# Sums per head, a fixed order of operations, and GpSimd for the lower words of the weights

## The chip, the cores and the metric

The kernel runs on one core of one Trainium2 chip. The metric is the device time of one launch in microseconds (us). All inputs lie in HBM and the output is written there.

## The reference

Two blocks run one after the other. The first is attention with a polynomial sketch: batch 4, 4 heads, 1088 tokens, 32 numbers a head, sketch size 8.

```python
def phi(x):
    a = np.einsum('rd,bhsd->bhsr', S1, x)
    b = np.einsum('rd,bhsd->bhsr', S2, x)
    return np.einsum('bhsi,bhsj->bhsij', a, b).reshape(*x.shape[:-1], r * r)
q_p, k_p = phi(q), phi(k)
num = np.einsum('bhsf,bhfd->bhsd', q_p, np.einsum('bhsf,bhsd->bhfd', k_p, v))
den = np.einsum('bhsf,bhf->bhs', q_p, np.sum(k_p, axis=2))[..., None] + 1e-06
x = (num / den)                       # then (B, S, H*D)
```

The second is a token mix with phases, on 128 channels:

```python
theta = x @ w_theta
y = w_tok_r @ (x * cos(theta)) + w_tok_i @ (x * sin(theta))     # over the tokens
u = x + y
out = u + np.maximum(u @ w_ch, 0.0)
```

The denominator can come close to zero, so the kernel carries it in two or more words of precision. The weights arrive as 64-bit floats.

## The kernel before, in words

Tokens lie on the 128 partitions, in 9 chunks. Nothing loops on the chip: the program lists some 990 operations with `op(engine, duration, function, writes, reads)` and the class `Layout` puts them in one order before anything is issued. An operation is one or a few instructions of one engine: P is TensorE (PE), V VectorE (DVE), A ScalarE (ACT), G GpSimd (POOL), S the queue of loads and stores on SyncE (SP). Each engine works off its own instructions in that order. In the kernel before, the order comes from a planner with durations, due times, a table `SHIFT` of corrections by stage, and buffer classes with reserves (L102 to L294). Where the planner foresees that PE stands, `issue` puts filler matmuls on an idle tile (`spin`, L458).

What is computed, with the names used below:

- **Weight rows.** The token weights are 17 rows of 128 x 1088 64-bit floats (`weight`, L671). A row is loaded into a `zs` buffer, ScalarE makes the upper word (L678) and the scaled and rounded lower word (L680), both into `big` buffers; VectorE shifts the upper word (L682) and adds the lower one (L684, shown as CUSTOM_DVE_ANT_0 at L407).
- **Keys** (`key_sums`, L700). For every batch k is split into a rounded bf16 part and a remainder. `sums` multiplies the rounded part with itself, `rest` the remainder with k (batch 0 in two products, batches 1 to 3 with k plus the rounded part, which an accumulating DMA has added up). All are 128 x 128 products over all four heads, though only the four 32 x 32 blocks on the diagonal are needed. Two or three products with the identity (`both`, `three`) add the transposed result.
- **The chain** (`chain`, L873; batches 0, 1, and 2 with 3 together). From the key products it makes the sum of the key features, in several words: `split`, `first`, `split_t`, `second`, a maximum, `cut`. Its result goes into the tables `mv` and `mf`, which `levels` (L1065) multiplies with q. `den` then makes the denominators, some ten VectorE steps a batch.
- **Values** (`kfeatures`, L793). The products of key features and v; batches 0 and 1 do two heads in one matmul (`sums`), batches 2 and 3 one head (`sums4`), which makes 128 x 32 pieces of the array.
- **Numerators** (`outputs_x`, L1144): an outer product on VectorE, transposes and matmuls on PE. They give x, then `theta`: rounding, Abs and two Sin on ScalarE, two steps on VectorE, which give z, the operand of the mix.
- **The mix.** Batches 0 and 1 multiply z with the 17 rows, 1088 columns a row (`mix_row`, L1260). Batches 2 and 3 share seven half-size products (`winograd`, L1300); their sums of weights come from VectorE (`asub`, `zsub`) and from accumulating DMAs that GpSimd issues (`aadd`, L1326). `balance` (L1233) gives the ratio of scale between these two batches. `finish` (L1286) multiplies with `w_ch`, adds, transposes and stores.

Of the kernel before, what the change touches and what calls it, by code (L numbers as in the profile page):

```python
# [29 lines left out]
MIX = (49.7, 1.87, 0.654, 0.0)  # L30
ROWS = (55.0, 3.96)
RPS = 4
EARLY = (2, 60.0, 4.0)
SHIFT = {
    "ac1": 1959.7, "ac2": -34.2, "ac3": 16.2, "ac4": 82.9, "acc1_0": 42.2, "acc1_1": -2320.9, "acc2_0": 31.2,
    "acc2_1": -673.1, "acc3_0": 5.8, "acc3_1": 932.8, "acc4_0": 3.9, "acc4_1": 16520.4, "acc5_0": 161.3,
    "acc5_1": 16109.1, "acc6_0": -223.6, "acc6_1": -1014.6, "acc7_0": 535.5, "acc7_1": -1181.2, "accl3_0":
    -35.5, "accl3_1": 15950.9, "blocks_k": 270.7, "blocks_m": 14976.6, "blocks_t": 353.2, "chain0": -7990.2,
    "chain1": -3583.6, "chain2": 70.5, "den0": -2490.2, "den1": 7.9, "den2": -6608.0, "den3": -20.6, "even":
    -4802.9, "first": -3782.9, "grid0": 274.3, "grid1": -1356.4, "grid2": -2521.6, "grid3": -5645.2, "kT0":  # L40
    -487.7, "kT1": -2.4, "kT2": -8729.0, "kT3": -4586.2, "keys0": -517.6, "keys1": -3965.9, "keys2": 1185.2,
    "keys3": 57.5, "kf0": -4478.9, "kf1": 31.3, "kf2": 427.4, "kf3": 16536.5, "kv0": -6047.2, "kv1": -6685.9,
    "kv2": -2098.9, "kv3": -8834.4, "kvb0": -4690.2, "kvb1": -2155.7, "kvb2": 600.6, "levels0": 1123.4,
    "levels1": -4027.2, "levels2": -2720.9, "levels3": -51.7, "loadh1": -3105.3, "loadh2": 24.7, "loadh3":
    -32.1, "loadk0": -4069.2, "loadk1": -8392.7, "loadk2": -1144.9, "loadk3": -5199.7, "loadq0": -7696.5,
    "loadq1": -6262.4, "loadq2": -958.3, "loadq3": 55.1, "loadv0": -5952.5, "loadv1": -912.1, "loadv2": -207.4,
    "loadv3": -1494.9, "m1_0": -1842.0, "m2_0": -13.3, "m2_1": 16313.2, "m3_0": 18317.8, "m3_1": 15711.6,
    "m4_0": 16151.7, "m4_1": 16888.8, "m5_0": 15826.2, "m5_1": 32.4, "m6_0": 182.9, "m6_1": 15250.5, "m7_0":
    16773.6, "m7_1": 15963.6, "mix0_0": 2883.6, "mix1_0": 16498.2, "mix1_1": -20.5, "mix1_2": 16164.9, "num0_0":
    -10062.4, "num0_1": -6861.6, "num0_2": -17390.2, "num1_0": -4679.4, "num1_1": -4010.3, "num1_2": 1566.7,  # L50
    "num2_0": -3.1, "num2_1": 15934.4, "num2_2": -4056.8, "num3_0": 15737.7, "num3_1": 35.0, "num3_2": -1483.3,
    "out0_0": -3691.3, "out0_1": 1196.2, "out0_2": -1707.0, "out1_0": 15899.8, "out1_1": 17081.6, "out1_2":
    -518.5, "out2_0_0": 6.6, "out2_0_1": 137.0, "out2_1_0": 16969.9, "out2_1_1": 16164.5, "out3_0_0": 16314.5,
    "out3_0_1": -978.2, "out3_1_0": 15740.8, "out3_1_1": 15780.8, "q00": -4645.6, "q01": 396.0, "q02": 43.0,
    "q03": -3238.5, "qT0": -372.8, "qT1": 531.2, "qT2": 18716.0, "qT3": 15783.1, "qscale0": -879.3, "qscale1":
    -7112.5, "qscale2": -116.9, "qscale3": -21.6, "rest0": -3460.7, "rest1": 15824.3, "rest2": -7.2, "rest3":
    -936.2, "row0": -32.5, "row1": -8124.5, "row10": -0.1, "row11": -1.8, "row12": -1.0, "row13": -6489.0,
    "row14": -2.1, "row15": 4.5, "row16": 6.0, "row2": -652.5, "row3": -35.3, "row4": -1008.6, "row5": -5.4,
    "row6": -5.0, "row7": -5.9, "row8": -2280.6, "row9": -7.6, "scaled": -2734.1, "sliced": 16062.8, "small":
    -5354.8, "square2": -5038.6, "sums0": 16352.5, "sums1": 2269.4, "sums2": 18.2, "sums3": 15743.7, "theta0_0":  # L60
    -4953.6, "theta0_1": -2793.7, "theta0_2": -11.6, "theta1_0": -4079.1, "theta1_1": -5573.0, "theta1_2":
    -2865.1, "theta2_0": -27.0, "theta2_1": -1634.0, "theta2_2": -41.0, "theta3_0": -677.3, "theta3_1": 133.0,
    "theta3_2": 382.0, "w2": -2254.2, "zc1": 1851.7, "zc2": 117.5, "zc3": 11.2, "zc4": 16233.0,
}
WARM = 0
FILL = 5.0
LOAD_LEAD = 60.0
RAW_LEAD = 30.0
# [4 lines left out]
PAIR = (2, 3)  # L73
SMALL = (2, 3)
# [7 lines left out]
ADD_FLY3 = 1.45  # L82
# [15 lines left out]
class Op:  # L98
    __slots__ = ("eng", "dur", "fn", "bufs", "pred", "succ", "due", "wait", "ready", "start", "end", "i", "lead", "rank", "lk", "fly", "stage", "chan")


class Layout:  # L102
# [9 lines left out]
    HURRY = 100.0  # L112
    LAND = 1.1
    STORE = 0.9
    RESERVE = {"big": 8, "zs": 2, "lv": 0, "hf": 1, "g3": 3, "g1": 2, "sm": 4, "ps": RPS}
    SLACK = {"P": 0.05, "V": 0.25, "A": 0.25, "G": 0.25, "S": 0.4}
# [10 lines left out]
    def op(self, eng, dur, fn, w=(), r=(), due=None, hold=(), lead=1e9, lk=0, fly=0.0, chan=0.0):  # L127
        o = Op()
        o.lk, o.fly, o.stage, o.chan = lk, fly + (chan + self.LAND if chan else 0.0), self.stage, chan
        o.i, o.eng, o.dur, o.fn, o.due = len(self.ops), eng, dur, fn, 1e9 if due is None else due  # L130
        o.succ, pred, o.lead = [], set(), lead
# [35 lines left out]
        for p in o.pred:  # L167
            self.ops[p].succ.append(o.i)
# [3 lines left out]
    def lag(self, o, t):  # L172
        if o.eng == t.eng:
            return o.fly + self.SAME[o.eng]
        return o.fly + self.LAT[o.eng] + (self.WAKE if t.eng == "G" else 0.0)

    def run(self):
        for o in reversed(self.ops):
            for s in o.succ:
                t = self.ops[s]  # L180
                o.due = min(o.due, t.due - t.dur - self.lag(o, t))
        for o in self.ops:
            o.due += SHIFT.get(o.stage, 0.0)
        return self.forward()

    def forward(self):
        ops = self.ops
        for o in ops:
            o.wait, o.ready, o.rank = len(o.pred), 0.0, o.due
            if o.eng in "VA" and any(b.cls == "ps" for b in o.bufs):  # L190
                o.rank -= self.HURRY
        slots = {c: [[0.0, None, i] for i in range(n)] for c, (n, _) in self.classes.items()}
# [3 lines left out]
        ready = {e: [o for o in ops if o.eng == e and not o.wait] for e in "PVAGS"}  # L196
        order, done = [], 0

        pending = {c: [] for c in self.classes}
        for b in self.bufs:  # L200
            b.left, b.slot, b.end = len(b.ops), None, 0.0
            if b.cls is not None:
                b.due = min(ops[i].due for i in b.ops)
                pending[b.cls].append((b.due, b.ops[0], b))
        for v in pending.values():
            v.sort(key=lambda x: x[:2])

        def place(o, loose):
            t = 0.0
            need = {}  # L210
            for b in o.bufs:
                if b.slot is None and b.cls is not None:
                    need.setdefault(b.cls, []).append(b)
# [1284 lines left out]
```

## Time and profile before

| | |
|---|---|
| median of 3 runs | 236.32 us (236.29 to 236.84) |
| the profiled execution | 235.85 us |
| its span, first to last instruction | 234.0 us |
| mean granted TensorE clock | 0.984 |
| instructions | 4153 |
| moved by DMA | 40.13 MB, 171 GB/s over the span |

The span is what the trace covers; the profiled execution's time lies 1.8 us above it. A row in a view names the line, the engine, the operation, what it writes and reads, the shape, and how many instructions there are. A helper's line stands for all who call it: every matmul of `mm` is L427, every `tensor_tensor` L407, every `tensor_scalar` L411. An f32 matmul leaves two records.

### The profile page before, as it was taken

How to read it: one execution, taken by the hardware profiler on the slowest of the kernel's cores; microseconds unless marked ns; L12 is line 12 of the kernel's file. 1: busy time of each engine (PE TensorE's matmuls, PEld its weight loads, DVE VectorE, ACT ScalarE, POOL GpSimd, SP SyncE). 2: the span in 40 equal slices, each digit the busy share in tenths (PEclk: the TensorE clock that was granted, in tenths of full speed). 3: DMA queues.
4: the chain of work that ended last, by engine and by line, in shares of the span. 5: the costliest groups of instructions: out<-in, count | busy, mean ns of one | idle time of the engine just before them, and what ended most of it. 6: DMA issues, size and time to landing. Idle time of an engine off the chain costs nothing.

```text
span 234.0 us, 4153 instructions
## 1 busy us (share of the span) xinstructions
PE 222.0 (95%) x1557; PEld 171.0 (73%) x1557; DVE 173.2 (74%) x356; ACT 114.4 (49%) x223; POOL 57.3 (25%) x110
## 2 busy tenths in 40 slices
PE   7899979999999998999999999999999999989980
PEld 3798969998787655765668676776868888767860
DVE  3599958998989999999458989778957862522241
ACT  3898648779699974997343103580026420000000
POOL 2299705110140000000277042000008664000000
PEclk9999979999999999999999999999999999999996
DMA  4999999997641797050097986010006999951124
GB/s 135 415 413 413 356 406 413 340 310 232 251 132 61 286 385 283 0 193 1 11 146 105 237 133 104 3 29 3 0 0 100 177 187 169 188 85 31 16 41 65
DMA packets 28035, 40.13 MB, mean 171 GB/s; under 512 B 19568, under 2 KB 20336, under 8 KB 25840
## 3 DMA queue, kind: packets, MB, share of 16 engines
q1 hardware_dynamic: 23168, 30.29, 38.3%
q0 software_dynamic: 4752, 9.57, 23.0%
q8 instruction: 12, 0.20, 0.3%
q14 instruction: 7, 0.06, 0.1%
q10 hardware_dynamic: 96, 0.01, 0.0%
HBM read 28.07 MB, written 2.23 MB: 129 GB/s over the span
## 4 chain that ended last, share of the span: by engine, by line
PE 58%; DMA 21%; DVE 8%; issue 5%; POOL 4%; ACT 1%; SPq 1%; POOLq 0%; ACTq 0%
PE ps L427 53%; DMA big<-q_l 6%; DMA zs<-big 5%; DMA zs<-w_tok 5%; DMA big<-hf 4%; POOL zs L1329 2%; DVE big L407 2%; PE ps L1170 2%; DVE big L411 1%; POOL big L1329 1%; PE ps L1203 1%; DVE lv L407 1%; PE ps L1050 1%; DVE zs L407 1%; DVE big L414 1%
## 5 line engine op out<-in xcount | busy, mean ns | idle before, releaser
L427 PE MATMUL ps<-big,zs 128*128 128x384 f32 (+3 forms) x348 | 100.0, 439 | 0.6 <-DVE big L407 0.6
L427 PEld LDWEIGHTS ps<-big,zs 128*128 128x128 f32 x348 | 64.6, 190 | 29.2 <-DVE big L407 2.0
L407 DVE CUSTOM_DVE_ANT_0 big<-big,big 128x2176 uint16<-128x2176 uint16 x17 | 21.9, 1286 | 0.7
L680 ACT ACTIVATE big<-zs 128x1088 int32<-128x1088 uint32 (+1 forms) x18 | 21.0, 1175 | 0.0
L421 POOL DMA_DIRECT2D g<-big x6 | 8.0, 1335 | 52.0 <-ACT g L1280 51.8
L678 ACT ACTIVATE big<-zs 128x1088 f32<-128x1088 f32 x17 | 20.5, 1220 | 0.1
L427 PE MATMUL ps<-big,big 128*128 128x128 f32 (+2 forms) x104 | 19.3, 316 | 0.5 <-DMA big<-hf 0.5
L427 PEld LDWEIGHTS ps<-big,big 128*128 128x128 f32 x104 | 15.4, 192 | 2.3 <-DMA big<-hf 0.8
L414 DVE SCALAR_TENSOR_TENSOR big<-ps,even,big 128x256 f32<-128x256 f32 (+1 forms) x10 | 5.0, 497 | 14.8 <-PE ps L427 14.8
L1329 POOL DMA_DIRECT2D big<-zs x8 | 7.0, 2064 | 32.1 <-PE ps L427 32.1
L407 DVE TENSOR_TENSOR zs<-ps,g 128x768 f32<-128x768 f32 (+2 forms) x20 | 12.2, 626 | 3.3 <-ACT g L1218 3.2
L427 PE MATMUL ps<-mf,big 128*128 128x96 f32 x72 | 14.3, 295 | 0.0
L411 DVE TENSOR_SCALAR big<-big 128x1088 int32<-128x1088 int32 x17 | 12.1, 719 | 0.4 <-ACT big L678 0.3
L427 PEld LDWEIGHTS <-hf 128*128 128x128 f16 (+1 forms) x144 | 11.1, 104 | 1.5 <-issue 0.9
L1141 ACT COPY big<-ps 128x288 f32<-128x288 f32 x8 | 2.6, 413 | 18.3 <-PE ps L427 18.3
L407 DVE TENSOR_TENSOR g<-lv 128x768 f32<-128x768 f32 x12 | 11.1, 946 | 0.1
L407 DVE TENSOR_TENSOR big<-big,hf 128x1152 f32<-128x1152 f32 x8 | 10.8, 1353 | 0.1
L427 PEld LDWEIGHTS ps<-mf,big 128*128 128x128 f32 x72 | 10.9, 191 | 0.0
L427 PE MATMUL ps<-mv,hf 128*128 128x96 f16 x108 | 10.5, 206 | 0.0
L427 PEld LDWEIGHTS ps<-w,big 128*128 128x128 f32 x72 | 9.3, 192 | 1.4 <-ACT big L1183 0.6
L427 PE MATMUL ps<-g,big 128*32 128x64 f32 (+1 forms) x216 | 8.9, 255 | 1.5 <-ACT sm L831 1.5
L427 PE MATMUL ps<-w,big 128*128 128x128 f32 x72 | 10.0, 277 | 0.0
(199 smaller groups left out, 410.3 us busy)
## 6 DMA issues: line engine op xcount, KB each, us to landing
zs<-w_tok SPq DMA_DIRECT2D x17, 1088.0 KB, 7.7
big<-k_l SPq DMA_DIRECT2D x7, 576.0 KB, 14.6
big<-q_l SPq DMA_DIRECT2D x4, 576.0 KB, 10.1
big<-v_l SPq DMA_DIRECT2D x4, 576.0 KB, 14.9
big<-big POOLq DMA_DIRECT2D x8, 272.0 KB, 7.0
big<-zs POOLq DMA_DIRECT2D x8, 272.0 KB, 8.9
zs<-big POOLq DMA_DIRECT2D x8, 272.0 KB, 10.3
big<-hf POOLq DMA_DIRECT2D x3, 576.0 KB, 9.2
```

The lines of the kernel that those rows point to most:

```text
L407: eng.tensor_tensor(out=o, in0=a, in1=b, op=f)
L411: (eng or V).tensor_scalar(out=o, in0=a, scalar1=s1, scalar2=s2, op0=op0, **kw)
L414: (eng or V).scalar_tensor_tensor(out=o, in0=a, scalar=s, in1=b, op0=op0, op1=op1)
L421: op("G", 0.9, lambda: G.dma_start(dst(), src(), accum_op=ALU.add), w, r, chan=chan)
L427: T.matmul(o, lhs, rhs, start=start, stop=stop, skip_group_check=True)
L678: op("A", 0.22 + n * 0.0009, lambda: A.activation(dfn(), words_of(raw(), n)[1].bitcast(F32), AF.Prelu, scale=2.0**-112, alpha=-(2.0**32)), ...
L680: op("A", 0.22 + n * 0.0009, lambda: A.activation(stp(), words_of(raw(), n)[0].bitcast(U32), AF.Copy, scale=2.0**-29), [stp], [raw])
L1050: T.transpose(tr()[:, i * P:(i + 1) * P], x()[:, g * GC + i].rearrange("p h d -> p (h d)"), ident())
L1141: op("A", act(NC * SQ), lambda i=i: A.copy(xt().rearrange("p (c q t) -> p c q t", q=NQ, t=SQ)[:, :, i], xps[i]()), cells(xt, 0, NC * P), [ ...
L1170: T.transpose(tr()[:, i * P:(i + 1) * P], qp()[:, i * H + 2 * n:i * H + 2 * n + 2].rearrange("p h i j -> p (h i j)"), ident())
L1203: T.transpose(x()[:, i], xs()[:, off + i * P:off + (i + 1) * P], ident())
L1329: op("G", 0.9, lambda i=i: G.dma_start(dst[0](i), x[0](i), accum_op=ALU.add), [dst[1](i)], [x[1](i)], chan=ADD_FLY3)
```

## The change

The diff has five parts.

1. **Order.** The planner with its due times is gone. A list `ORDER` of all 993 operation numbers, in the order of their calls, is followed as it stands; the remaining model in `run` serves the choice of buffers and the filler.
2. **Key sums per head.** `sums` and `rest` make four 32 x 32 products a chunk. The products with the identity go; `split` transposes the blocks on VectorE instead.
3. **Compact chain.** The intermediate results hold 8 columns a batch where there were 32, since each head lies on its own partitions; `first` becomes narrow matmuls, the mask is applied later, in `norms` and `cut`.
4. **Values.** Batches 0 and 1 also take one head a matmul.
5. **Lower words.** For weight rows 4 to 16 GpSimd scales and rounds the lower word, for the others ScalarE still does.

In `balance`, VectorE's two maxima become two squares with a sum on ScalarE. Loads are queued in another order, and so are the accumulating DMAs. `QBLOCK` is empty, so its branch is not taken.

```diff
+LOW = tuple(range(4, 17))
...
     def run(self):
-        for o in reversed(self.ops):
-            for s in o.succ:
-                t = self.ops[s]
-                o.due = min(o.due, t.due - t.dur - self.lag(o, t))
-        for o in self.ops:
-            o.due += SHIFT.get(o.stage, 0.0)
-        return self.forward()
...
+        seq = [int(x) for x in ORDER.split()]
...
+        self.order = [ops[i] for i in seq]
...
+        if low:
+            op("G", 0.06 + n * 0.00115, lambda: ts(stp(), words_of(raw(), n)[0].bitcast(U32), 2.0**-29, ALU.mult, eng=G),
+               [stp], [raw], lk=1)
+        else:
+            op("A", 0.22 + n * 0.0009, lambda: A.activation(stp(), words_of(raw(), n)[0].bitcast(U32), AF.Copy,
+                                                         scale=2.0**-29), [stp], [raw])
...
-        t = kk[b] = buf("ps", (4, HD), F32, "kk")
+        t = kk[b] = buf("ps", (3, D), F32, "kk")
+
+        def heads(i, x, y, start, stop):
+            for h in range(H):
+                e = slice(h * D, (h + 1) * D)
+                mm(t()[e, i], x[:, e], y[:, e], start, stop)
+
         for c in range(NC):
-            op("P", 0.056, lambda c=c: mm(t()[:, 0], kb()[:, c], kb()[:, c], c == 0, False), [(t, "l")], [kb])
+            op("P", 0.1, lambda c=c: heads(0, kb()[:, c], kb()[:, c], c == 0, False), [(t, "l")], [kb])
...
-            def both():
-                mm(t()[:, 2], g()[:, 1], ident(), False, False)
-                mm(t()[:, 2], ident(), g()[:, 1], False, True)
...
+            def split(b=b, e0=e0, e1=e1):
+                x = kg[b, 0]()
+                V.transpose(out=x[:, 2], in_=x[:, 1])
+                tt(V, x[:, 1], x[:, 1], x[:, 2], ALU.add)
+                if not KDMA[b]:
+                    tt(V, x[:, 1], x[:, 1], x[:, 3], ALU.subtract)
+                stt(e0(), x[:, 1], kg[b]()[:, 0:1], x[:, 0], ALU.add, ALU.add)
+                stt(e1(), e0(), kg[b]()[:, 0:1], x[:, 0], ALU.subtract, ALU.subtract)
+                tt(V, e1(), x[:, 1], e1(), ALU.subtract)
...
+        def norms():
+            V.tensor_reduce(out=m4()[:, 2, 0:nb], in_=np_()[:, 0], axis=AX.X, op=ALU.add, apply_absolute_value=True)
+            tt(V, m4()[:, 0].rearrange("p (b h) -> p b h", h=H), bc(m4()[:, 2, 0:nb], 2, h3), bc(hm(), 1, h3), ALU.mult)
...
-            vop(NC * P, lambda j=j, b=b: V.tensor_reduce(out=even()[:, j:j + 1], in_=xT[b](), axis=AX.X, op=ALU.max,
-                                                         apply_absolute_value=True), [(even, j)], [xT[b]])
+            op("A", act(NC * P) + 0.1, lambda j=j, b=b, junk=junk: A.activation(junk(), xT[b](), AF.Square,
+                                                                                accum_out=even()[:, j:j + 1]),
+               [junk, (even, j)], [xT[b]])
```

## The prediction

> **What bounds the kernel now.** I read the busy shares first.
>
> ```profile
> PE 222.0 (95%) x1557; PEld 171.0 (73%) x1557; DVE 173.2 (74%) x356; ACT 114.4 (49%) x223; POOL 57.3 (25%) x110
> ```
>
> TensorE looks like the bound, so the time by stage came next. I cut the span at 72.13 (first row of the token mix of batch 0, from the timeline of PE), at 104.04 (end of the second large `zs<-ps,g` product of batch 1 on VectorE: its z is there but for one group) and at 228.65 (last matmul). Columns: PE, PEld, DVE, ACT, POOL busy, clock, DMA.
>
> ```profile
> 0.00:36.00 36.00, 32.35 (x265) 26.67 (x267) 26.25 (x76) 24.14 (x59) 19.01 (x51) 0.95 0.93 358
> 36.00:72.13 36.13, 35.47 (x462) 31.64 (x456) 33.51 (x70) 30.33 (x63) 8.83 (x17) 1.00 0.79 271
> 72.13:104.04 31.91, 31.08 (x129) 19.86 (x130) 31.38 (x53) 26.33 (x39) 0.00 (x0) 1.00 0.55 208
> 104.04:228.65 124.61, 123.10 (x709) 92.79 (x708) 81.08 (x157) 33.61 (x66) 29.51 (x42) 1.00 0.51 84
> 228.65:234.05 5.40, 0.01 (x1) 0.00 (x0) 0.94 (x2) 0.00 (x0) 0.00 (x0) 0.62 0.41 64
> ```
>
> Two regimes. From 36 to 104 us VectorE is busy 64.9 of 68.0 us and PE 66.6. From 104 on VectorE has a third of its time free and PE is busy 123.1 of 124.6. But before 104 a part of PE's time is filler: 8.0 us is L459, matmuls on `idle`. So up to 104 us PE has slack that VectorE has not; after it PE alone counts. The end is therefore **the time at which z of batch 1 is there, plus the PE work still left then**. The waits agree: in 36 to 104 us VectorE waits for others about 1.4 us in all, beyond gaps between its own instructions.
>
> **The edits on PE.** The timeline of PE, start and length of a run of records (an f32 matmul has two records):
>
> ```profile
> 20.16 1.53 PE L427 MATMUL ps<-g,big 128*64 128x128 f32 x24
> 52.50 0.54 PE L427 MATMUL ps<-g,big 128*32 128x64 f32 x24
> 45.81 1.33 PE L427 MATMUL ps<-hf 128*128 128x128 bf16 x18
> 54.98 2.25 PE L427 MATMUL ps<-big,big 128*128 128x128 f32 x18
> ```
>
> From each start to the next run's: 1.46, 0.48, 1.17 and 2.09 us.
> - Value sums of batches 0 and 1: two groups in 1.46 us, 0.73 each; in the per-head form 0.45 (0.48, and 0.44 where two groups run together). Six groups: -1.7.
> - Rounded key products: 36 at 0.065 = 2.3 us, become 144 narrow bf16 ones. The second row gives 0.020 us a record, the 32*32 rows (64 in 1.53) 0.024: 2.9 to 3.5 us. +0.9.
> - Remainder products: 27 at 0.232 and 18 at 0.225 = 10.3 us, become 180 narrow f32 ones, 360 records, at 0.020: 7.2 us. Bounds 3.6 (half the columns, half the time) and 9.2, with 0.1 for each of some 20 places where the array changes between forms: three transposes take 0.33 among their like and 0.47 before a narrow group (52.03 to 52.50). -3.1.
> - Nine products with the identity go (0.77 + 3 x 0.50): -2.3. The first chain product, 4 x 0.46, becomes 64 records at 0.024: -0.3.
>
> Sum -6.5 us, bounds -3 to -11. All of it lies before 104 us, where PE is not the last: I count it at **nothing but the waits it shortens**. The Trainium skill, "TensorEngine Tiling (Array Packing)", Tiling Modes, says that a change of tiling mode drains the array; the 0.14 us above agrees in sign, and by it, too, the cost falls where PE has slack.
>
> **The edits on VectorE, up to z of batch 1.** Work there is 26.25 + 33.51 + 31.38 = 91.1 us. I numbered the operations by their calls and read the list `ORDER` engine by engine: up to the same point it holds 14 finished weight rows (before: 5 additions up to 69.93, 9 after: 14). Differences: the third numerator product of batch 1 comes in (+0.9), the rounding of q of batch 2 goes out (-0.7); `split` gets a transpose and an addition on 32 columns but all its steps shrink (five steps at 0.22, the pitch of the 128x32 steps at 35.95 to 37.06, for 0.98; one more for batch 0): +0.7; the masked copy leaves `split_t` (-1.1); `norms` and `cut` get one step each (+0.9); constants +0.2. **92.0 us.**
>
> Its idle time up to there is 104.04 - 91.14 = 12.9 us. 6.5 of it is in the first 12 us (windows of 6 us) and waits for the first loads and the small weights: stays. 2.3 is the wait for PE at 32.8: PE stood for `sm`, ACT before it for `big<-q_l`; in `ORDER` that square stands elsewhere: goes. The other 4.1 I halve, since the chains lose an ACT-PE round trip each and ACT loses the lower words (1.2 us a row, 13 rows; ACT was busy 26.33 of 31.91 us in the third stretch). **8.5 us.**
>
> **The lower words on GpSimd.** The trace has no GpSimd operation of this size. By the nearest rows:
>
> ```profile
> 1.34 0.28 POOL masks.py:199 TENSOR_SCALAR_AFFINE_SELECT ident<-ident 128x128 f32<-128x128 f32 x1
> 12.02 1.43 POOL L407 TENSOR_TENSOR sq<-sq,s 128x8 f32<-128x8 f32 x1
> 12.04 1.35 DVE L407 TENSOR_TENSOR big<-big,hf 128x1152 f32<-128x1152 f32 x1
> 23.33 1.03 POOL L407 TENSOR_TENSOR pbd<-psc,hm 128x128 f32<-128x128 f32 x2
> 7.75 0.88 DVE L411 TENSOR_SCALAR hf<-big,sm 128x1152 bf16<-128x1152 f32 x1
> 23.90 1.56 DVE L411 TENSOR_SCALAR hf<-big,sm 128x1152 bf16<-128x1152 f32 x1
> ```
>
> An 8-element GpSimd step (0.2 alone) lasts until VectorE's addition ends; and VectorE's rounding, 0.88 alone, takes 1.56 where GpSimd is at work. So the two exclude each other while VectorE reads two operands, or one at the double rate, from SBUF. Length of one row: 0.28 - 0.19 for 128 elements is 0.7 ns each, 0.95 us for 1088; with two operands (0.515 - 0.19 for 128) 2.5 ns, 2.9 us. One operand is read here: I take 0.95. Eleven rows stand before z of batch 1 in `ORDER`: 10.5 us. Cover: VectorE's steps fed from PSUM (five of 0.5 and five of about 0.95 for theta, the reductions of `den1`, 1.1) and 2 us of idle time, 10.4 us; not all of it stands next to a row, I take two thirds, 7.0. **3.5 us** of VectorE is lost; bounds 0 (all covered) and 13 (1.2 a row, nothing covered). If the operation waits instead, the row's addition on VectorE waits behind it, and all behind that: the same price.
>
> The Trainium skill, "GPSIMD Engine Reference", Key points, says that GpSimd's SBUF interfaces are shared with VectorE's two-input and two-port instructions; the rows above agree. Its Performance pitfalls give some 1.9 cycles an element for steps up to 8 bytes, by which a row would be 1.72 us (an estimate from that page) and the loss 12 us after the same cover.
>
> **Sum.** z of batch 1 at 92.0 + 8.5 + 3.5 = 104.0 us, as now. Left before: 234.05 - 104.04 = 130.0 us. Of that, the third group's transposes and numerator of batch 1 (1.5 us at 115.6) and 0.7 of a mix row (80 records, 13.3 rows before; 14 in `ORDER`; 1.81 us each) are done earlier: -2.8. PE's wait of 0.9 us for the `zs<-big` additions at 206.7 I take as gone, since `ORDER` spreads product 7 among product 3 and puts product 4 last. The two VectorE maxima (1.35 each) that become ACT squares (1.16) lie after 104 and cost nothing while PE is full. 126.3 us left: span 230.3; the profiled execution lies 1.8 over its span (235.85), the median 0.5 over that: **232.5 us**.
>
> **Rivals.**
> 1. GpSimd hides fully and the waits before 104 nearly vanish (idle 7.5): 92.0 + 7.5 + 126.3 = 225.8, some 228 us. For it: both ACT and PE get slack at once. Against it: VectorE's steps there are mostly of the excluding kind.
> 2. **Slower: the shared port becomes the bound.** Each row on GpSimd holds VectorE's next step for most of its length, between 60 and 105 us. It decides from a loss of 7.0 us on (0.65 a row): then the time is 236. At 1.2 us a row, a quarter covered, 9.9 us are lost: 239. For it: the row of 1.56 us, and that VectorE has 3% idle there. Against it: the short form of one row, and that ACT's waits, the other side of the exchange, were real.
> 3. Nothing shows: the second half is reordered too, and the accumulating transfers (8 x 272 KB, 7 to 10 us to landing, q0 23%) come late for products 5, 3 and 7; with 3 us of PE waiting there the gain is given back: 235.5. For it: PE already waits once for them. Against it: DMA is half idle after 104 us.
>
> **Numbers.** Forecast 0.47 (its own range 230 to 235), rival 1 0.22, rival 2 0.20, rival 3 0.11. The range 226.5 to 238.5 leaves out the ends of rivals 1 and 2. A measurement of this kernel tells about 0.3% (0.7 us) from no change; faster than that: forecast and rival 1 and a little of 3, 0.70; within: 0.10; slower: 0.20.
>
> **What would show it.** Right: z of batch 1 near 104 us, more filler on PE or idle PE before it, VectorE above 95% from 36 to 104 us with steps of 0.7 and 1.3 us stretched where GpSimd works, ACT clearly freer, PE full afterwards. Wrong: a row on GpSimd far from 0.95 us; z of batch 1 before 100 (rival 1) or after 107 (rival 2); PE standing after 104 us (rival 3); or VectorE's rows of the same size unchanged beside a busy GpSimd, then there is no exclusion and the loss is zero.

## The result and the profile after

The changed kernel takes 247.57 us in the median of four runs (246.35 to 253.6), the kernel before 236.31 beside it: 1.048 times as long, interval 1.0425 to 1.0526. The change makes the kernel 11 us slower; 232.5 was forecast. One run of the four, 253.6 us, lies 2.9% above the fastest and is left out of the ratio. The profiled execution took 248.12 us, its span is 246.3.

The page of after: the busy shares, the granted clock in 40 slices, and three groups of instructions (busy us, mean ns of one, then the idle time ahead of the group and what ended it).

```profile
PE 223.5 (91%) x2017; PEld 170.3 (69%) x2017; DVE 178.4 (72%) x366; ACT 103.2 (42%) x219; POOL 103.1 (42%) x121
...
PEclk9999555599999999679999999999999999999998
...
L350 POOL TENSOR_SCALAR big<-zs 128x1088 int32<-128x1088 uint32 x13 | 47.1, 3625 | 24.7 <-DVE big L346 10.3
L346 DVE CUSTOM_DVE_ANT_0 big<-big,big 128x2176 uint16<-128x2176 uint16 x17 | 22.5, 1341 | 2.1 <-POOL big L350 2.0
...
L350 DVE TENSOR_SCALAR big<-big 128x1088 int32<-128x1088 int32 x17 | 17.7, 1041 | 0.0
```

A row on GpSimd takes 3.6 us, not 0.95. VectorE's shift of a row went from 719 to 1041 ns, its addition from 1286 to 1341. And the clock, near full before, stands at half in slices 5 to 8, from 25.7 to 49.6 us.

The same cuts as in the prediction, in after: the first row of the mix of batch 0 starts at 72.51 us, z of batch 1 is there at 117.25, and the last matmul ends at 239.7. Columns: PE, PEld, DVE, ACT, POOL busy, clock, DMA share, GB/s.

```profile
0.00:36.00 36.00, 28.68 (x522) 25.67 (x522) 27.64 (x85) 23.94 (x61) 17.68 (x52) 0.86 0.93 358
36.00:72.51 36.51, 35.73 (x572) 29.40 (x571) 29.04 (x63) 25.02 (x53) 13.28 (x9) 0.81 0.60 208
72.51:117.25 44.74, 38.41 (x233) 23.78 (x234) 43.39 (x61) 25.24 (x47) 36.24 (x16) 0.92 0.53 200
117.25:240.72 123.47, 120.73 (x695) 91.45 (x693) 78.35 (x160) 28.97 (x62) 35.89 (x47) 1.00 0.50 85
```

The loss is in the third line: the stretch that took 31.9 us takes 44.7. VectorE is busy 97% of it and GpSimd 81%, PE only 86%. The timelines of GpSimd and PE show what each waits for there:

```profile
78.14 10.62 POOL L350 TENSOR_SCALAR big<-zs 128x1088 int32<-128x1088 uint32 x3 [0.77 <-PE ps L945]
...
89.50 14.15 POOL L350 TENSOR_SCALAR big<-zs 128x1088 int32<-128x1088 uint32 x4
```

```profile
92.55 3.92 PE L366 MATMUL ps<-big,zs 128*128 128x384 f32 x12 [1.50 <-DVE big L346]
102.98 6.19 PE L366 MATMUL ps<-big,zs 128*128 128x384 f32 x12 [1.93 <-DVE big L346]
```

Seven rows stand back to back on GpSimd for 25 us, and PE, with the mix of batch 0 in hand, waits for finished rows (the addition, L346). From 100.8 to 107.6 us the clock is at half once more (slices 17 and 18): the twelve records at 102.98 take 6.19 us where those at 92.55 took 3.92.

**A sum for the kernels below.** As in the prediction, the span is cut where z of batch 1 is there, and the time up to there is divided into VectorE's busy and idle time. All but the medians are read from the windows and timelines of the profiled execution of each run (us). "The same" means after with early filler and one more edit; "old order" is the order of the kernel before:

| kernel | z of batch 1 | VectorE busy + idle | left after it | span | median |
|---|---|---|---|---|---|
| before | 104.0 | 91.1 + 12.9 | 130.0 | 234.0 | 236.3 |
| forecast of after | 104.0 | 92.0 + 8.5 + 3.5 lost | 126.3 | 230.3 | 232.5 |
| after | 117.3 | 100.1 + 17.2 | 129.0 | 246.3 | 247.6 |
| after, filler early | 114.5 | 100.1 + 14.4 | 128.2 | 242.7 | 244.5 |
| the same, rows on ScalarE | 114.0 | 90.5 + 23.5 | 126.4 | 240.4 | 241.2 |
| the same, rows of 8 columns | 102.2 | 89.9 + 12.3 | 126.6 | 228.8 | 233.5 |
| old order, new operations, rows on ScalarE | 106.2 | 90.5 + 15.7 | 130.2 | 236.4 | 239.4 |
| old order and operations as above, aimed filler | 105.1 | 90.8 + 14.2 | 129.8 | 234.9 | 237.6 |

### The profile page after: what moved, and what is told of

It is laid out like the page before. It is cut to its first block, busy times and chain, and to the rows that moved or that the text cites. A ratio compares the mean times of both kernels' runs of the same rounds, so it can differ in the third digit from the quotient of the medians.

```text
span 246.3 us, 5094 instructions
## 1 busy us (share of the span) xinstructions
PE 223.5 (91%) x2017; PEld 170.3 (69%) x2017; DVE 178.4 (72%) x366; ACT 103.2 (42%) x219; POOL 103.1 (42%) x121
## 4 chain that ended last, share of the span: by engine, by line
PE 66%; DVE 18%; POOL 5%; issue 4%; ACT 3%; DMA 1%; SPq 1%; DVEq 0%; ACTq 0%; POOLq 0%
PE ps L366 58%; DVE big L346 5%; POOL big L350 5%; DVE big L350 3%; DVE g L346 3%; PE ps L751 2%; PE ps L993 2%; DVE sm L346 2%; PE ps L1146 1%; PE ps L1113 1%; DVE sm L353 1%; DVE zs L346 1%; PE ps L398 1%; SPq L1240 1%; DMA st<-s_t 1%
## 5 line engine op out<-in xcount | busy, mean ns | idle before, releaser
L366 PE MATMUL ps<-big,zs 128*128 128x384 f32 (+3 forms) x348 | 105.1, 448 | 6.3 <-DVE big L346 5.9
L350 POOL TENSOR_SCALAR big<-zs 128x1088 int32<-128x1088 uint32 x13 | 47.1, 3625 | 24.7 <-DVE big L346 10.3
L346 DVE CUSTOM_DVE_ANT_0 big<-big,big 128x2176 uint16<-128x2176 uint16 x17 | 22.5, 1341 | 2.1 <-POOL big L350 2.0
L346 DVE TENSOR_TENSOR zs<-ps,g 128x768 f32<-128x768 f32 (+2 forms) x20 | 12.5, 629 | 11.4 <-PE ps L1146 7.5
L350 DVE TENSOR_SCALAR big<-big 128x1088 int32<-128x1088 int32 x17 | 17.7, 1041 | 0.0
L366 PE MATMUL ps<-mf,big 128*128 128x96 f32 x72 | 17.2, 336 | 0.0
L1026 ACT COPY lv<-ps 128x480 f32<-128x480 f32 x12 | 6.4, 559 | 20.4 <-DVE zs L1070 11.8
L366 PE MATMUL ps<-big,big 128*32 128x32 f32 (+2 forms) x320 | 14.7, 234 | 0.0
L366 PEld LDWEIGHTS <-hf 128*32 128x32 bf16 (+1 forms) x252 | 12.2, 109 | 2.6 <-issue 1.6
L366 PE MATMUL ps<-sbk,g 128*128 128x64 f32 x72 | 13.0, 337 | 0.2 <-ACT g L754 0.2
L346 DVE TENSOR_TENSOR g<-lv 128x768 f32<-128x768 f32 x12 | 13.1, 1110 | 0.1
L366 PEld LDWEIGHTS ps<-big,big 128*32 128x32 f32 (+1 forms) x320 | 10.9, 133 | 3.1 <-issue 1.7
L366 PEld LDWEIGHTS ps<-sbk,g 128*128 128x128 f32 x72 | 12.0, 250 | 0.7 <-ACT g L754 0.4
L353 DVE SCALAR_TENSOR_TENSOR big<-ps,even,big 128x288 f32<-128x288 f32 (+1 forms) x10 | 4.8, 490 | 10.3 <-PE ps L366 10.2
L1158 ACT ACTIVATE g<-g 128x384 f32<-128x384 f32 x12 | 6.2, 518 | 12.3 <-DVE g L353 12.3
L346 DVE TENSOR_TENSOR big<-big,hf 128x1152 f32<-128x1152 f32 x8 | 10.7, 1350 | 0.0
```

The lines of the kernel that those rows point to most:

```text
L346: eng.tensor_tensor(out=o, in0=a, in1=b, op=f)
L350: (eng or V).tensor_scalar(out=o, in0=a, scalar1=s1, scalar2=s2, op0=op0, **kw)
L353: (eng or V).scalar_tensor_tensor(out=o, in0=a, scalar=s, in1=b, op0=op0, op1=op1)
L366: T.matmul(o, lhs, rhs, start=start, stop=stop, skip_group_check=True)
L1026: op("A", act(480), lambda g=g, lp=lp: A.copy(lv().rearrange("p l (c n) -> p l c n", n=HR)[:, :, g * GC:(g + 1) * GC], lp().rearrange("p c ...
L1158: op("A", act(GW), lambda cs=cs: A.activation(cs()[:, 0], cs()[:, 1], AF.Abs), [(cs, 0)], [(cs, 1)])
```

## The experiments

Theory A: the 13 rows on GpSimd are what costs. Theory B: the changed list starts the filler at 48.9 us instead of 1.3, TensorE's clock stays at half, and that costs. Theory C: the list itself costs. Ratios are against the kernel before on the same chip.

### Rows and filler, one at a time and together

All rows back on ScalarE is one line, `LOW = ()`. Early filler moves the list's numbers 0 and 1 (GpSimd's memset, the first 11 filler products) to its front and adds three filler products to each group of key transposes (the filler that the plan adds, one product in after, is off where early filler is on):

```
+     0 1 4 5 6 7 2 8 11 12 30 ...
...
             def trs(g=g, tr=tr):
+                fill(tr(), 3)
                 for i in range(GC):
```

> The changed kernel, but all 17 lower words on ScalarE, at the same places of the list (13 operations move from GpSimd's queue to ScalarE's). Theory A, the rows on GpSimd (3.6 us each in the trace of the changed kernel, and VectorE's steps stretched beside them) cost most of what was lost: VectorE's stretch from the first mix row to z of batch 1 goes from 45 us back to 34 to 37 us, the time to 237 to 240 us. Theory B, the clock (granted 0.5 from 25.7 to 49.6 us, where the list has no filler) costs most: the time stays above 243 us and the first mix row stays at 72 us. Theory C, the list itself orders badly whatever the engines do: above 243 us with a full clock from 50 us on and PE waiting for other things than rows.

> The changed kernel with filler matmuls: the memset of the idle tile and eleven of them stand first in the list, into a PSUM bank that is given back at once, and three stand before each of the twelve groups of key transposes, into the bank that the transposes then overwrite. Theory A: the clock recovers and the first mix row comes some 5 us sooner, but the rows on GpSimd still set z of batch 1, so that the time moves by at most 4 us: 243 to 248 us. Theory B: the time falls by 8 us or more, below 240 us. If the clock still stays at 0.5 for over 10 us, filler is not what it lacks.

> Both edits: all lower words on ScalarE, and the filler matmuls. Theory A and B together explain the loss, and the cheaper PE and chain work then show: 230 to 234 us, faster than before. If the list or the per-head sums cost something of their own (theory C): 236 us or more.

Measured: 244.04 us without GpSimd rows (ratio 1.038, 1.030 to 1.046), 244.48 with early filler (1.037, 1.031 to 1.043), 241.19 with both (1.023, 1.017 to 1.030). By the medians each edit alone gains 3 us or so, with an interval that overlaps that of after (1.0425 to 1.0526), and the two together gain 6.4, clear of noise. The first run lies above the range of A; its stretch from the first mix row to z of batch 1 takes 40.9 us, not 34 to 37. The second lies in A's range and above B's. The third is not the 230 to 234 of A and B together, but lies where C put it: some 5 us remain that the two edits don't explain. Either the list costs (C), or the rows cost on ScalarE as well. For the second the trace speaks. With both edits, ScalarE is busy 11.97 of the 12 us from 60 to 72, VectorE 5.71 and PE 8.47, and VectorE waits 5.69 us for a lower word from ScalarE (L621):

```profile
60.00:72.00 12.00, 8.47 (x230) 6.99 (x229) 5.71 (x9) 11.97 (x20) 2.19 (x5) 0.96 0.37 93
...
70.77 1.29 DVE L346 CUSTOM_DVE_ANT_0 big<-big,big 128x2176 uint16<-128x2176 uint16 x1 [5.69 <-ACT big L621]
```

In the kernel before the same window has ScalarE nearly as full, but VectorE at 10.96 and PE at 11.92:

```profile
60.00:72.00 12.00, 11.92 (x109) 9.75 (x107) 10.96 (x23) 11.21 (x24) 3.70 (x7) 1.00 0.47 172
```

The list was laid out with these rows elsewhere; put back on ScalarE they stand among the steps that VectorE needs for z.

### The kernel before with GpSimd rows

The other way round: the kernel before, its planner left to order it, with the lower words of rows 4 to 16 on GpSimd.

```
+LOW = tuple(range(4, 17))
...
+        if low:
+            op("G", 0.06 + n * 0.00115, lambda: ts(stp(), words_of(raw(), n)[0].bitcast(U32), 2.0**-29, ALU.mult, eng=G),
```

> The kernel before with one part of the change alone: the lower words of rows 4 to 16 on GpSimd; its planner plans them at 1.31 us each. Theory A: the rows take 3 us and more here too and VectorE's steps are stretched: 243 to 252 us. If the rows do harm only in the new list, or because of the low clock: 234 to 238 us.

Measured: 261.73 us (ratio 1.112, 1.102 to 1.121). Above the range of A: the step alone, without any of the cut products, costs some 26 us where the order was planned with rows of 1.31 us. A row takes 3.36 us, and z of batch 1 is there at 124.1 us: VectorE is busy 98.2 us up to there (before: 91.1) and idle 25.9 (12.9).

### The new operations in the old order, and rows cut to 8 columns

Two runs split the rest. One takes the changed operations (all 17 rows on ScalarE) in the order that the planner of before gave to their counterparts; its edit is another `ORDER`. The other takes the new list with early filler, and shrinks the step to 8 columns, so that it costs neither GpSimd nor ScalarE much; VectorE's addition, as long as before, reads these columns over and over, and the kernel leaves the rest of these lower words out:

```
-            op("G", ..., lambda: ts(stp(), words_of(raw(), n)[0].bitcast(U32), 2.0**-29, ALU.mult, eng=G),
+            op("G", ..., lambda: ts(stp()[:, 0:8], words_of(raw(), 8)[0].bitcast(U32), 2.0**-29, ALU.mult, eng=G),
```

> The operations of the changed kernel (key sums per head, compact chain, value sums per head, squares for the two maxima), but in the order that the planner of the kernel before gave to their counterparts, with the filler from the start as before, and with all 17 lower words on ScalarE. Theory C (the new order costs, not the operations): 229 to 233.5 us, so 2.5 to 7 below before, since the matmuls that were cut are still cut. Theory D (the new operations cost more on VectorE and ScalarE than they save on TensorE): 236 or more.

> The changed kernel with the filler at the start and ahead of the key transposes (as in the run with both), and the 13 GpSimd rows cut to 8 columns each; the addition reads these 8 columns over and over, so the lower words of these rows are left out and the output differs. GpSimd and ScalarE are then both free of these 13 steps. Theory A (the rows, on whichever engine, were what held the order up): 229 to 233 us, 8 or more below the run with both. Theories C and D: 237 us or more, within 4 of the run with both.

Measured: 239.37 us (ratio 1.0135, 1.009 to 1.018) and 233.49 us (0.989, 0.983 to 0.996; its four runs took 230.6, 232.9, 234.1 and 239.1 us, and the profiled one is the first). The first lies in the range of theory D (the new operations cost VectorE and ScalarE more than they save TensorE), the second just above that of A and below those of C and D. Without the rows' length the new list is the faster one, by the medians 11.0 us below the same list with GpSimd rows and 7.7 below it with ScalarE rows: theory A, with the addition that the rows cost on either engine. Theories C and D fall with it: it is the old order that gains nothing from the cut products. The windows of the 8-column run:

```profile
36.00:66.89 30.89, 27.78 (x538) 22.06 (x535) 27.00 (x60) 24.69 (x51) 8.25 (x14) 0.94 0.79 271
66.89:102.18 35.29, 35.29 (x242) 22.62 (x234) 34.79 (x61) 24.47 (x45) 6.32 (x10) 1.00 0.60 230
```

The mix starts at 66.9 us, 5.6 before after's, and from there to z of batch 1 PE stands nowhere. From the rows of the sum above: with GpSimd rows VectorE is busy 10.2 us longer up to there (100.1 against 89.9) and idle 2.1 longer; with ScalarE rows it is busy as long as without (90.5), and idle 11.2 us longer. Two prices, two ways: in this list, rows on GpSimd slow VectorE's own steps, and rows on ScalarE make it wait.

### The row step by itself

A kernel with none of the computation: GpSimd runs the step twice alone, then other forms of it, then beside VectorE; TensorE meanwhile runs stretches of products.

```
    for _ in range(2):
        stride2_scaled(step)                              # uint32, every second word, to int32
...
    for _ in range(18):
        V.tensor_tensor(out=vec, in0=vec, in1=oth, op=ALU.add)
    for _ in range(3):
        stride2_scaled(step)
```

> No part of the computation; zeros are stored. GpSimd does the row step alone: twice from every second word of 128x1088 as uint32 to int32 (the step of the change), twice from a contiguous tile as uint32 to int32, twice from every second word as float32, twice contiguous float32; then three times beside VectorE additions (two int32 inputs) and three times beside VectorE shifts (one input). Theory A1 (the step is long by itself): 2.9 us or more alone, whatever VectorE does, and the form that costs is told by the other three. Theory A2 (it is held up by VectorE): 1.0 to 1.9 us alone and 3 or more beside VectorE. TensorE meanwhile runs seven stretches with no wait between them: float32 128x128 products, narrow 32-column float32 products, a stretch like the query levels (three float16 96-column and one float32 96-column product), bfloat16 384-column filler, then the level stretch, the narrow and the 128x128 ones again. Theory B1 (a busy TensorE lifts the clock, whatever it does): granted clock at full within 7 us of the start and then all the way. Theory B2 (short products don't lift it, the filler does): half until the filler stretch, full behind it.

Its timeline of GpSimd, five lines of it (from every second word as uint32; float32 of every second word; contiguous uint32; contiguous float32; and the first again beside VectorE's additions):

```profile
6.54 3.03 POOL L81 TENSOR_SCALAR step<-raw 128x1088 int32<-128x1088 uint32 x1 [6.12 <-DMA raw<-w_tok]
9.66 3.04 POOL L81 TENSOR_SCALAR flt<-raw 128x1088 f32<-128x1088 f32 x1
...
19.00 2.96 POOL L81 TENSOR_SCALAR cont<-step 128x1088 int32<-128x1088 uint32 x1
22.04 2.97 POOL L81 TENSOR_SCALAR zero<-flt 128x1088 f32<-128x1088 f32 x1
...
37.83 3.45 POOL L81 TENSOR_SCALAR step<-raw 128x1088 int32<-128x1088 uint32 x1
```

Theory A1 holds: the step is 3.0 us long by itself, 2.7 to 2.8 ns an element, and neither type nor stride matters much (2.96 to 3.04). Beside VectorE it takes 3.4. What it does to VectorE, by the 18 additions (min, median, max ns):

```profile
L96 DVE CUSTOM_DVE_ANT_0 vec<-vec,oth x18: 1291/1293/2191, 31.3 to 59.0; 128x2176 uint16<-128x2176 uint16 x18
```

While the six GpSimd rows run, the trace has additions of 2.12 to 2.19 and of 1.29 us in turn, six long ones, one to a row; behind the last row all take 1.29. **A row costs VectorE 0.86 us here** (2.15 less 1.29). Twelve rows start before z of batch 1 in after: 12 x 0.86 = 10.3, and 10.2 is what VectorE is busier there than in the 8-column run. The price a row is the same, but other steps pay it. Of the 17 shifts 11 touch a GpSimd row and take 1.22 us in the mean, six do not and take 0.72; up to z of batch 1 the shifts pay 4.5 of the 10.2 us. The products `g<-lv` pay 1.9, the additions, 14 of them, only 1.0, and small steps the rest. So why the price a row agrees so well isn't shown. The shifts that were meant to run beside rows in this run came too late and tell nothing.

The clock in this run: it rose some 4.5 us behind the first product, stayed full through the 128x128 products, fell to half at 26.2 us in the narrow ones, and came back 4.7 us after the level stretch began (45.4 to 50.0). So neither B1 nor B2 fits. The narrow ones were not a busy stretch, though: PE stood 1.5 to 2.5 us after every 128 records, waiting for nothing that the profile shows.

### What the narrow products wait for

```
    narrow(300)
    mixed(40)
...
    for i in range(17):
        ...
        SY.dma_start(busy[i % 6], w_tok[i])
    ...
    narrow(500)
```

> No part of the computation; zeros are stored. TensorE alone, with key values in place of the zeros of the run with rows alone: 128x128 products, the level stretch, narrow products, levels, filler, narrow, filler, and then 500 narrow products beside the loads of all 17 weight rows. Theory F (TensorE is fed instructions in pages of 256, and narrow products use a page up in 1.9 us or less while the next takes some 3.5): stretches of 128 records with stands of 1.5 to 2.5 us in the narrow stretches, one page fetched per stand, and longer stands (3 or more) beside the loads; half clock follows each narrow stretch that stands. Theory N (the stands have another cause): no fetched page lies next to the stands, or they are the same beside the loads. Clock: if the values matter, the level stretch stays at half for more than 7 us behind the narrow one; if not, it is at full within 7 us.

PE in a narrow stretch by itself (first two lines) and beside the loads of 17 weight rows:

```profile
46.98 1.93 PE L85 MATMUL pb<-f32a 128*32 128x32 f32 x128 [2.45 <-issue]
50.70 1.51 PE L85 MATMUL pb<-f32a 128*32 128x32 f32 x97 [1.80 <-issue]
...
101.24 1.93 PE L85 MATMUL pb<-f32a 128*32 128x32 f32 x128 [5.46 <-issue]
107.98 1.94 PE L85 MATMUL pb<-f32a 128*32 128x32 f32 x128 [4.81 <-issue]
```

128 records are 256 instructions with their weight loads, and the page's queue list has

```profile
q8 instruction: 19, 0.31, 1.0%
```

19 packets of 16 KB, 64 bytes for each of 256 instructions. In the trace one such packet starts 2.5 to 2.9 us ahead of each resumption; the packets are 3.7 to 4.1 us apart by itself and 6.1 to 6.7 beside the loads. That is theory F: TensorE's instructions come in pages, and narrow products use a page up (1.3 to 1.9 us) faster than the next arrives. The Trainium skill, "Runtime: NRT & Kernel Launch", Instruction fetch mechanics, describes the refill in 16 KiB blocks, as seen here, and says that it is mostly hidden; here it isn't. Clock: the level stretch came back to full 3.2 us after its start (52.2 to 55.4) with key values in place of zeros, so the values aren't what held it down.

### Do the stands, or the products, undo the gain in the old order?

The run in the old order has a stand of 3.33 us at 18.0 (`issue`), two of 0.9 at 51 and 52, one of 0.5 at 57, and half clock for 13.7 us ahead of the mix (15.9 to 22.7, 53.4 to 56.8, 60.3 to 63.7). The three that end with `issue` (18.0, 52.4, 57.3) end 2.2 to 2.5 us behind the start of an instruction packet, as theory F has it. Two edits to this run: each set of four narrow key products replaced by one with 32 columns (three heads then get another head's sums, so this kernel leaves work out); and value sums two heads at a time again.

```
-            for h in range(H):
-                e = slice(h * D, (h + 1) * D)
-                mm(t()[e, i], x[:, e], y[:, e], start, stop)
+            mm(t()[:, i], x, y[:, 0:D], start, stop)
```

```
-            op("P", 0.5, sums4, [acc], [kp, vx])
+            op("P", 0.5, sums4 if b in SMALL else sums, [acc], [kp, vx])
```

> The run with before's order, with each set of four narrow 32x32 key products replaced by one product of 128 rows and 32 columns (three of four heads get another head's sums, so the output differs): 45 x 3 fewer matmuls for batch 0 and fewer for the others, nothing else moved. Theory F (stands for instructions, and the half clock behind them, cost the run with before's order its gain): 235 to 237 us, 2.5 to 4.5 below it. Theory D (the compact chain on VectorE and ScalarE costs): 238.5 or more, within 1 us of it.

> The run with before's order, with the value sums of batches 0 and 1 two heads at a time again, as in the kernel before (18 products of 128 columns in place of 36 of 64 a batch). Prediction's step (per-head value sums save 1.7 us): 241 us. Theory F: 238 to 239.5 us, no loss, as the stands at the value sums of batch 0 (0.9 and 0.9 us) go with them.

Measured: 241.33 us (1.018, 1.010 to 1.027) and 244.54 us (1.033, 1.026 to 1.040). Both lie above what theory F expected. With a quarter of the instructions the `issue` stands are gone, and yet the kernel is no faster: 2 us slower by the medians, which isn't clear of noise. Pair sums cost 5 us, three times the 1.7 that the prediction gave them; but in that run the `issue` stands got longer (3.91 us at 18.7, 2.68 at 52.8), so it doesn't show what they cost. Both traces show half clock between 54 and 71 us, 10.2 and 13.6 us of it (6.8 between 53 and 64 in the run they start from, none in before), much of it where PE works without a gap towards the mix.

### What the rows are worth to the kernel before

The kernel before, its order untouched, 13 lower-word steps on ScalarE cut to 8 columns.

```
-        op("A", ..., lambda: A.activation(stp(), words_of(raw(), n)[0].bitcast(U32), AF.Copy,
...
+        m = 8 if low else n
+        op("A", ..., lambda: A.activation(stp()[:, 0:m], words_of(raw(), m)[0].bitcast(U32), AF.Copy,
```

> The kernel before with the lower words of the same 13 rows cut to 8 columns on ScalarE, the rest and the order as they are (these words are left out, the output differs). It shows what freeing ScalarE of these 13 steps is worth at most to the kernel before, without the other parts. Theory A (the 13 steps, wherever they run, are what counts, and the cut products bring little): 230 to 233.5 us, no slower than the changed kernel with 8-column rows. Prediction's view (13 steps taken off ScalarE bring some 0 to 2 us, the products 6): 234 to 236 us.

Measured: 235.93 us (0.996, 0.992 to 1.000). That is the prediction's view, and A's range is missed: taking 13 steps of 1.2 us off ScalarE brings the old order next to nothing (z of batch 1 at 102.5 for 104.0). The engine that the change relieves was not one that the old kernel waited for. It also is the fair match for the 8-column run of the new list: both leave the same words out, and 0.989 against 0.996 is all that list and cut products gain, which isn't clear of noise.

### The clock as a cause

Filler is the line `fill(tr(), 3)` above, at the key transposes and in one run at the query transposes too; the kernel before without filler is

```
-FILL = 5.0
+FILL = 0.0
...
-    first = op("P", 3.2, lambda: [spin() for _ in range(11)], ...
+    first = op("P", 3.2, lambda: [spin() for _ in range(1)], ...
```

> The run with before's order, with three filler products ahead of each of the 12 groups of key transposes. Theory K (the cut products leave TensorE standing in the first 72 us, the clock falls to half for some 14 us ahead of the first token-mixing product, and that takes the gain back): half clock of 7 us or less ahead of it, and 232 to 236 us. Theory D (VectorE and ScalarE pay for the compact chain): 239 us or more, as filler can only add.

> The same with three filler products ahead of each of the 12 groups of query transposes too (0.5 us each at full clock, so 6 us more of TensorE work). Theory K: within 2 us of the run with filler at the keys, below 238. Theory D: 240 us or more.

> The kernel before, in its own order, with one filler product in all in place of its 56 or so. Theory K: half clock of 20 us or more ahead of the first token-mixing product, and 240 to 246 us. Theory D (the clock of the first stretch is not what counts there): 235 to 238 us.

> The kernel before, in its own order, with three more filler products ahead of each of the 12 groups of key transposes. Before has half clock for only 8 us in its first 72. Theory K: 235 to 239 us, little to gain (3.4 us of half clock at most) against up to 6 us of filler on a TensorE that is full already. If it falls below 234, filler alone gains, and a gain of the kernel with cut products and filler would not be the products'.

Measured: 241.71 us (1.030, 1.027 to 1.033) and 246.12 (1.044, 1.038 to 1.049) for the old order with new operations; 236.05 (1.004, 1.002 to 1.006) and 237.62 (1.010, 1.008 to 1.013) for the kernel before. Theory K falls in this form: it expected 232 to 236 and below 238 for the first two, 240 to 246 for the third. The kernel before without filler loses 0.9 us, though its products take up to twice their later length for the first 17 us. Filler at the key transposes still left 6.8 us of half clock ahead of the mix (61.1 to 67.9) and cost 2.3 us by the medians. What is left of K is a guess: half clock counts only where PE is the last, in the stretch ahead of the mix.

The next two test that, with no planned filler (`FILL = 0`), and with filler only near the stands from 49 to 60 us:

```
+                fill(tr(), 5 if b == 2 else 0)      # query transposes
...
+            fill(pt(), 4 if bs == (1,) else 0)      # ahead of the chain's sum
```

> The run with before's order and the new operations, without the planned filler (one filler product in all instead of 56). Theory K2 (half clock between 54 and 72 us, behind stands of TensorE, is what costs; at the start it costs nothing): half clock of 7 us or more in that stretch and 236 to 240 us, as with the planned filler. Theory L (filler that the plan set between late products holds TensorE up, 7 us of it between 18 and 27 us): 233 to 235.5 us. Theory D (the compact chain on VectorE and ScalarE): 238.5 to 240 us, whatever the clock.

> The same, with five filler products ahead of each of the three groups of query transposes of batch 2 (near 49 to 55 us) and four ahead of the one sum of the chain of batch 1 (near 60 us): 3 us of filler where TensorE stands. Theory K2: half clock of 3.4 us or none between 54 and 72 us, and 231.5 to 235 us, 2 or more below the run without filler. Theory L: within 1 us of the run without filler, or above it. Theory D: 239 us or more.

Measured: 237.84 us (1.012, 1.006 to 1.018) and 237.61 (1.008, 1.005 to 1.012). Without the planned filler the run lies in K2's range and above L's; the 1.5 us that it gains by the medians aren't clear of noise (1.012 for 1.0135). The aimed filler does to the clock what it was meant to do in the stretch ahead of the mix (old order with planned filler, then with aimed filler):

```profile
PEclk9985999997799999999999999999999999999998
```

```profile
PEclk9999999999999999999999999999999999999997
```

and that gains nothing that can be told from noise: 237.6 is above K2's range (231.5 to 235), and within 1 us of the run without filler, as theory L has it. The clock ahead of the mix may have a part in the 239.4 and in the two runs before; no run shows how large. One hole is left: the second clock row shows 9 from the start, but products take nearly twice as long up to some 31 us there (three transposes 0.85 us at 29.5, 0.50 at 32.4). With the clock full from then on, the new operations in the old order are still 0.8% slower than before. The sum says why they gain nothing there: VectorE is busy 90.8 us up to z of batch 1, in before 91.1, and what is left after it is 129.8, in before 130.0. The products that were cut stand in neither.

### Rows shared

`LOW = tuple(range(4, 17, 2))`: seven rows on GpSimd, six on ScalarE, in the new list with early filler.

> The changed kernel with filler at the start and the key transposes, with seven of the 13 rows (4, 6, ..., 16) on GpSimd and six on ScalarE. With all 13 on GpSimd it was 244.5, with all on ScalarE 241.2, with 8 columns 233.5 us. Theory Q (each engine's queue fills up, and the half that it can hide costs nothing): 234 to 237.5 us. Theory R (any row that stands ahead of the others in a queue delays the order, the prices add): 242 to 243.5 us, between the two.

Measured: 239.35 us (1.013, 1.006 to 1.019), below both unshared runs (244.5 and 241.2) and between the two theories' ranges. The prices don't simply add, and they don't vanish. No version that does all the work beats the kernel before.

## Why the prediction was wrong, point by point

**What bounds it.** The frame held. The end is z of batch 1 plus the PE work left then: in the old order what is left is 129.7 to 130.2 us in nine kernels, 130.3 and 131.3 in the two with most filler, and 136.4 with GpSimd rows, in the new list 126.4 to 129.0.

**Sum, 126.3 us left.** Right. The new list with rows on ScalarE has 126.4, with 8 columns 126.6. In after it is 129.0: PE stands for late rows behind z of batch 1 too (0.96 us at 127.4 and 0.21 at 122.5, among others).

**The edits on PE, -6.5 us, counted at nothing.** Right in the count, wrong in the size. In the 8-column run eight f32 records of the remainder products take 0.065 us, 0.008 a record; 360 are 2.9 us for 7.2 in the sum and 3.6 as its lower bound. A set of 36 bf16 records takes 0.25, four are 1.0 for 2.9 to 3.5. By these rows the cut is some 13 us (7.4 + 1.3 + the 2.3, 1.7 and 0.3 as estimated), outside the bounds of 3 to 11; the stands for instructions take some of it back. That work on VectorE hides it was right: in the old order it gives no gain at all. With the list 126.6 us are left after z instead of 130.0, since mix work is done ahead of it.

**VectorE's work, 92.0 us.** In the 8-column run it is 89.9: 2 too many.

**VectorE's idle time, 8.5 us.** Wrong: 12.3 in the 8-column run, 12.9 in before. I halved 4.1 and dropped 2.3 because chains and ScalarE get shorter; the run of before with 8-column rows shows that ScalarE's relief brings z of batch 1 forward by 1.5 us there, and the list had its own waits.

**The lower words on GpSimd, 0.95 us a row and 3.5 us lost. This is the step that failed.** The row is 3.0 us by itself and 3.6 in the kernel. I took the length of an affine select per element (0.7 ns) because it has one operand; the two-operand row in the same fence gave 2.5 ns and 2.9 us, and that came out right, though a row of 128 columns with two operands need not tell of this one. By the Trainium skill's "GPSIMD Engine Reference", Performance pitfalls, the estimate was 1.72 us a row; the measured row is 1.7 times that. The exclusion was right in kind. Its size is 0.86 us of VectorE a row, times 12 rows, 10.3 us (10.2 in the busy time) for 3.5; the cover of 7 us was not there. And rows of 3 us and more come late: 2.1 us more of VectorE's idle time. Together 8.8 of the 16.0 us by which the span was missed.

**A step that the prediction left out: the filler.** It took it as given ("more filler on PE"). In the list the numbers 0 and 1 stand behind 229 others. So after has its first PE instruction at 6.0 us; its products take up to twice their length until 15.4 us (three transposes 0.88 to 0.90, then 0.53, though the clock row shows 9), and the clock is at half from 25.7 to 49.6. Early filler gains 3.1 us with GpSimd rows and 2.9 without, by the medians.

**The account.** z of batch 1 came at 117.3 for 104.0, 13.3 late: VectorE's own work -2.1; slowed steps +6.7 (10.2 for 3.5); idle time +8.7, of it 2.8 the missing filler, 2.1 late rows, 3.8 the waits that I had taken as gone. Left after it +2.7. In all +16.0, the span's 246.3 for 230.3.

**Rivals.** The second came true in kind, "the shared port becomes the bound": two of its signs were seen, a row far from 0.95 us and z of batch 1 after 107. Its price, 9.9 us lost, is close to the 10.2 measured by luck, for it comes from rows of 1.2 us with three quarters uncovered, and the rows took 3.6 and cost 0.85 each. It had 0.20, because I gave the short row the weight; and its 239 us lacked the filler and the waits. Rival 1 (GpSimd hides) is out. Rival 3 (late transfers) plays no part: after z of batch 1 PE waits for no DMA.

**What stays open.** In after the clock stays at half for 24 us while PE is busy all the time, through the whole level stretch; alone, the same stretch brought it back in 4.7 and 3.2 us. No run tells why. The waits of 3.8 us that the list adds were not taken apart. And why six rows on ScalarE plus seven on GpSimd cost less than either whole is told only by its time.

## What to carry to other kernels

An operation on a new engine is first priced from the slowest row that resembles it per element, or run by itself; here the row that was set aside was right within 5%. Where two engines exclude each other, count what each step takes from the other engine (0.86 us here) and multiply by the steps on the path, before crediting any cover. And when one explicit list replaces a planner, read where its first and its filler operations stand, and which engine's queue each moved step now stands ahead of: the same 13 steps were nearly free on ScalarE in the old order (235.9 us without their length, 236.2 with it) and cost 7.7 us there in the new one.

## What the runs showed of the hardware

- GpSimd's one-operand step on 128x1088 takes 2.96 to 3.04 us for uint32 and float32, strided or contiguous, and 3.4 beside VectorE's two-input additions, of which one in two then takes 2.15 for 1.29 us.
- Narrow products (32 columns) run at 0.008 us a record in short stretches, but long stretches of them are fed one page of 256 instructions every 3.4 to 4.1 us, and every 6.1 to 6.7 us beside loads at some 420 GB/s.
- Which stand of TensorE lowers the clock can't be read from these traces. In the run with one product it fell at 14.6 us behind 3.4 us with 2.87 busy, in after at 25.7 behind 3.4 us with 2.60 busy; but in after it stayed full at 87.1 behind 3.4 us with 2.09 busy.
- In the kernel before, products at up to twice their length for the first 17 us cost 0.9 us in all: TensorE isn't the last there.
